# Strided products, copies and sums of zeros appended behind the last result, on four engines

## The chip, the core and the metric

The kernel runs on one core of a Trainium2 chip. The metric is the device time of one execution in microseconds; the figure given for a kernel is the median of its runs. A profiled execution of the same program supplies the trace that is read below. Five engines work side by side, each with its own queue in program order: PE (TensorE: matmuls, with a weight load, PEld, ahead of each), DVE (VectorE), ACT (ScalarE), POOL (GpSimd) and SP (SyncE, which issues the transfers). They wait for each other through semaphores.

## The reference

Two layers of width 1024 over a sequence of 2048 are computed from separate inputs and laid side by side. The first is attention with 32 heads of 32, the second a Fourier mixing by four given DFT matrices:

```
qkv = transpose(reshape(x @ wqkv))                 # 3, heads, sequence, 32
p   = softmax(q @ k.T * 32 ** -0.5)
a   = reshape(transpose(p @ v)) @ wo

re  = x @ dft_hid_re.T
im  = x @ dft_hid_im.T
b   = dft_seq_re @ re - dft_seq_im @ im

out = concatenate([a, b], axis=-1)                 # 1, 2048, 2048
```

All inputs and the output are fp32.

## The kernel before

Every dense product is made of 128 x 512 tiles. An fp32 operand is split into a high and a low part in the type fp32r, which TensorE multiplies faster than plain fp32, and a product is the sum of three: high by high, low by high, high by low. `halves` makes the two parts (the high part by a copy on DVE, L501, or on ACT, L499; the low part by a subtraction on POOL or DVE, L504). `group` issues the matmuls of one accumulation (L414) into a PSUM tile that `bank` takes from the pools `psD` (tile name `pd`) or `psT`. The larger products are cut by a seven-product scheme, with sums and differences of blocks made by `fetch` (L479).

The order of all engines is written out by hand. The class `Plan` simulates the engines with given costs while the program is being emitted: every operation is an `Op` with an engine, a cost, what it waits for and a rank, and `start` emits it into its engine's queue when the simulated engine comes free. The main loop at the end of `tile_mha_fnet_kernel` draws PE's work from four sources (scores, transposed scores, products with v, and the dense groups that fill what is left); the other engines follow in `others`. All of this stands in a `manual_schedule`, so each engine's queue has exactly the order in which instructions were emitted. The semaphores are put in afterwards from the tiles that instructions read and write. The plan also keeps POOL's operations and those DVE operations that are marked `two` (copies between SBUF tiles, and sums with two SBUF operands) apart from each other where it can.

SBUF is handed out by name. The pool `big` has 20 places `slot0` to `slot19` of 128 x 2 x 512 floats; taking a place again waits for all that read or wrote its previous tile. The pool `pre` has, among others, three places with the tag `c` of 128 x 512 floats. The PSUM pools have two tiles each: `psD` and `psT` of 512 columns and `psS` of 1024, which held score tiles during attention.

At the end stands `project_end`. It finishes the last fourth of the output projection: for each of 16 row blocks n and both halves e of the columns, a group of six matmuls over the last two chunks g of the contraction, whose result `total` adds to a partial sum (L1474, on DVE, one operand in SBUF and one in PSUM) and stores (L1479). The stores go out on SP's queue. The very last result is added and stored in two halves, the second of them on ACT's queue. In this part the places are used so: with BASE = 10 the offset o is 5, so the weights `ENDS_B[6, 0]`, `[6, 1]`, `[7, 0]` and `[7, 1]` lie in slots 1, 2, 3 and 4, the activations `ENDS_A` in slots 16 to 19 and 5 to 8, and the partial sums of block n, two per place, in slots 9, 10, 11, 0 and 12 to 15 in turn. Slot 0 thus holds those of blocks 3 and 11. A store uses one of eight semaphores ("lanes") in turn; a later one of the same lane waits for the earlier to land.

After the main loop the rest of the plan is run out, the manual order is closed, and `op_pool` makes sure that the late pools exist. Then every engine drains, SP waits for all transfers, and the engines meet (all recorded with the line L2162).

Two other places are spoken of below: the warm-up at the start (L377 to L379), eight products of zeros into a PSUM tile that nothing reads, and the softmax sums of a head on DVE (L1923 to L1927), a short chain in which each operation reads what the one before it wrote.

```
def halves: high: copy raw -> hi (DVE L501 or ACT L499)
            low:  raw - hi       (POOL or DVE L504)
def total:  acc + psum (DVE L1474), store (SP, the last half ACT, L1479)
```

Of the kernel before, what the change touches and what calls it, by code (L numbers as in the profile page):

```python
# [8 lines left out]
F32 = mybir.dt.float32  # L9
F32R = mybir.dt.float32r  # L10
AF = mybir.ActivationFunctionType
ALU = mybir.AluOpType
# [4 lines left out]
P = 128  # L17
# [6 lines left out]
NB = 512  # L24
# [198 lines left out]
def kernel(  # L223
# [12 lines left out]
    nc = tc.nc  # L236
# [35 lines left out]
    big = ctx.enter_context(tc.tile_pool(name="big", bufs=1, side="right"))  # L272
# [13 lines left out]
    pre = ctx.enter_context(tc.tile_pool(name="pre", bufs=1, reuse_waits="tile"))  # L286
# [34 lines left out]
    psS, psT, psD = (pools[n] for n in ("psS", "psT", "psD"))  # L321
# [60 lines left out]
    op = pl.op  # L382
# [1425 lines left out]
    def op_pool():  # L1808
        if "op" not in late:
            att().release()  # L1810
            qk0.release()
            late["atl"].release()
            late["oph"] = ctx.enter_context(tc.tile_pool(name="oph", bufs=1, side="right", reuse_waits="tile"))
            late["op"] = ctx.enter_context(tc.tile_pool(name="op", bufs=1, reuse_waits="tile"))
        return late["op"]
# [238 lines left out]
    while nf < len(fills) or any(place[n] < len(s) for n, s in streams.items()):  # L2054
# [18 lines left out]
        for n, (o, h, k) in heads.items():  # L2073
# [8 lines left out]
            if n == "V":  # L2082

                near = any(m in heads and heads[m][0].left == 0 and heads[m][0].ready + LATE < pl.now + NEAR and not (m == "S" and held) for m in "ST")
# [29 lines left out]
        if ok:  # L2114
            n = min(ok)[1]
# [10 lines left out]
        t = min(times)  # L2126
# [3 lines left out]
    while True:  # L2130
        pl.others()
        t = pl.next_time()
        if t > 1e17:
            break
        pl.now = max(t, pl.now + 1e-3)
    guard.__exit__(None, None, None)
    op_pool()

# [27 lines left out]
```

## Time and profile before

| | us |
|---|---|
| median of 3 runs | 2922.96 |
| lowest, highest run | 2922.64, 2923.09 |
| the profiled execution | 2929.45 |
| its span, first to last instruction | 2927.7 |
| PE busy | 2904.0 |
| DVE busy | 2386.5 |
| ACT busy | 2373.3 |
| POOL busy | 1241.3 |

The granted TensorE clock was 0.999 of full speed. The profiled execution is 6.5 us above the median, and 1.75 us of it lie outside the span. In the views below, the timeline gives the start in microseconds from the start of the span, the duration, the engine, the line, the operation with its output and inputs, its count, and in brackets the idle time of the engine before it with what ended it. Neighbouring instructions of one kind are merged into one row. The view of one line or one tile gives the count, the shortest, median and longest duration in nanoseconds, and the first and last start. An engine name with a q (SPq, ACTq) is the engine's sequencer: waits, drains and the issue of transfers.

### The profile page before, as it was taken

To read this page: it belongs to the slowest core of one execution; us is meant where nothing else is said; L and a number is where in the kernel's file an instruction comes from. 1 tells how busy PE (TensorE), PEld (TensorE's weight loads), DVE (VectorE), ACT (ScalarE), POOL (GpSimd) and SP (SyncE) were. 2 spreads that over 40 slices of the span, in tenths; PEclk is the share of its full clock that TensorE was granted. 3 is DMA by queue.
4 is the path that set the end of the run, shared out by engine and by line. 5 is a ranking of instruction groups with operands and counts; after the bars stand their busy time and mean duration, and the time that the engine had idled before them with its cause. 6 is when DMAs were issued, how large, how long until landed. Compare 5 with 4: busy or idle time off the path is not lost.

```text
span 2927.7 us, 47039 instructions
## 1 busy us (share of the span) xinstructions
PE 2904.0 (99%) x14728; PEld 2107.2 (72%) x14728; DVE 2386.5 (82%) x3251; ACT 2373.3 (81%) x4509; POOL 1241.3 (42%) x975
## 2 busy tenths in 40 slices
PE   9999999999999999999999999999999999999999
PEld 8887776777667777777676677667667777777777
DVE  7679888788788887788888898888988788788745
ACT  5348898888888888988999898898889888888741
POOL 2325534142233433337655456666675352243200
PEclk9999999999999999999999999999999999999999
DMA  9989978697789988867899776887876665677558
GB/s 345 349 298 328 314 225 272 222 346 269 268 289 339 309 297 287 291 213 218 291 348 333 226 223 216 276 272 229 271 229 208 204 180 181 193 246 226 188 191 287
DMA packets 485844, 768.18 MB, mean 262 GB/s; under 512 B 120382, under 2 KB 153406, under 8 KB 485470
## 3 DMA queue, kind: packets, MB, share of 16 engines
q1 hardware_dynamic: 485452, 765.04, 79.4%
q8 instruction: 119, 1.95, 0.3%
q14 instruction: 129, 1.06, 0.1%
q10 hardware_dynamic: 144, 0.13, 0.0%
HBM read 511.74 MB, written 253.25 MB: 261 GB/s over the span
## 4 chain that ended last, share of the span: by engine, by line
PE 75%; DMA 4%; DVE 1%; ACT 1%; SPq 0%; issue 0%; POOL 0%; DVEq 0%; ACTq 0%; POOLq 0%
PE pd L414 34%; PE psT L1975 14%; PE pd L1994 13%; PE psS L1853 13%; PE psT L414 2%; ACT psS L1862 1%; DVE negm L1859 1%; DMA qs<-m_d 1%; DMA slot<-in_ct 0%; DMA g<-in_ct 0%; DMA hl<-ha_d 0%; ACT pt L1979 0%; DMA m_d<-lt 0%; DMA ha_d<-slot 0%; DMA g<-g_d 0%
## 5 line engine op out<-in xcount | busy, mean ns | idle before, releaser
L414 PE MATMUL pd<-slot,hl 128*128 128x512 f32 x5028 | 1446.7, 390 | 4.2 <-DMA hl<-ha_d 1.4
L1979 ACT ACTIVATE pt<-psT 128x512 f32<-128x512 f32 x2048 | 1191.5, 668 | 260.7 <-PE psT L1975 258.5
L1859 DVE TENSOR_REDUCE negm<-psS 128x1 f32<-128x1024 f32 x1024 | 1240.7, 1221 | 198.3 <-PE psS L1853 190.1
L1862 ACT ACTIVATE psS<-psS,negm 128x1024 f32<-128x1024 f32 x1024 | 1189.2, 1161 | 47.4 <-DVE negm L1859 44.5
L414 PEld LDWEIGHTS pd<-slot,hl 128*128 128x128 f32 x5028 | 943.6, 188 | 204.8 <-DVE negm L1859 2.7
L1975 PE MATMUL psT<-qs,ks 128*128 128x512 f32 x2048 | 802.4, 395 | 4.4 <-DMA qs<-m_d 3.2
L1975 PEld LDWEIGHTS psT<-qs,ks 128*128 128x128 f32 x2048 | 382.2, 188 | 160.0 <-issue 53.0
L1853 PE MATMUL psS<-ks,qs 128*128 128x512 f32 x1552 | 473.1, 391 | 4.2 <-ACT psS L1862 4.2
L1994 PE MATMUL pd<-pt,vt 128*32 128x512 f32 x4096 | 460.9, 596 | 1.2 <-DVE e L723 0.9
L1853 PEld LDWEIGHTS psS<-ks,qs 128*128 128x128 f32 x1552 | 289.5, 188 | 69.1 <-ACT psS L1862 11.0
L504 POOL TENSOR_TENSOR slot<-raw,slot 128x512 fp32r<-128x512 f32 x153 | 196.2, 1291 | 316.1 <-DVE slot L501 116.6
L1994 PEld LDWEIGHTS pd<-pt,vt 128*32 128x32 f32 x4096 | 123.4, 110 | 285.1 <-issue 268.3
L504 POOL TENSOR_TENSOR slot<-slot,slot 128x512 fp32r<-128x512 f32 x183 | 234.3, 1292 | 206.1 <-DVE slot L501 54.5
L1862 ACT ACTIVATION_READ_ACCUMULATOR psS<-psS,negm 128x1 f32 x1024 | 287.0, 280 | 0.0
L504 POOL TENSOR_TENSOR hl<-raw,hl 128x512 fp32r<-128x512 f32 x122 | 156.8, 1289 | 257.4 <-DVE hl L501 84.7
L479 POOL TENSOR_TENSOR raw<-raw,g 128x512 f32<-128x512 f32 x119 | 153.3, 1291 | 226.6 <-ACT pt L1979 31.3
L414 PE MATMUL pd<-slot,slot 128*128 128x512 f32 x780 | 210.6, 389 | 0.1
L414 PEld LDWEIGHTS pd<-slot,slot 128*128 128x128 f32 x780 | 146.4, 188 | 30.9 <-DVE e L723 0.4
L1853 PE MATMUL psS<-ks,qx 128*128 128x512 f32 x496 | 151.0, 394 | 3.3 <-ACT psS L1862 3.2
L479 DVE TENSOR_TENSOR raw<-raw,g 128x512 f32<-128x512 f32 x141 | 103.3, 738 | 23.6 <-DMA g<-in_ct 6.6
L1853 PEld LDWEIGHTS psS<-ks,qx 128*128 128x128 f32 x496 | 91.7, 188 | 34.6 <-issue 9.2
L479 POOL TENSOR_TENSOR slot<-slot,slot 128x512 f32<-128x512 f32 x79 | 102.1, 1302 | 27.5 <-DVE slot L479 11.3
(140 smaller groups left out, 2167.6 us busy)
## 6 DMA issues: line engine op xcount, KB each, us to landing
hl<-ha_d SPq DMA_DIRECT2D x134, 512.0 KB
slot<-in_ct SPq DMA_DIRECT2D x144, 256.0 KB
qk_d<-e SPq DMA_DIRECT2D x52, 512.0 KB
qs<-qk_d SPq DMA_DIRECT2D x128, 192.0 KB
ks<-qk_d SPq DMA_DIRECT2D x128, 192.0 KB
raw<-g_d SPq DMA_DIRECT2D x96, 256.0 KB
ha_d<-hl SPq DMA_DIRECT2D x42, 512.0 KB
raw<-in_ct SPq DMA_DIRECT2D x80, 256.0 KB
```

The costliest lines, as they stand in the source:

```text
L414: nc.tensor.matmul(box["ps"], a[1]((a[0].hi, a[0].lo)[u]()), b[1]((b[0].hi, b[0].lo)[v]()), start=k == 0, stop=k == n - 1)
L479: (nc.gpsimd if e == "POOL" else nc.vector).tensor_tensor(out=dest(), in0=dest() if a is None else a.get(), in1=other["q"] if "q" in other ...
L504: (nc.gpsimd if e == "POOL" else nc.vector).tensor_tensor(out=lo(), in0=raw(), in1=f(hi()), op=ALU.subtract)
L1853: nc.tensor.matmul(p[:, i * NB : i * NB + NB], (QX[0] if own else QS[h % 2])[:, qt * P : qt * P + P], KS[h % 2][:, c * 1024 + i * NB : c * ...
L1859: nc.vector.tensor_reduce(out=ST["negm"][:, c, qt : qt + 1], in_=box["p"], axis=AX.X, op=ALU.max, negate=True)
L1862: nc.scalar.activation(box["p"], box["p"], AF.Exp, bias=ST["negm"][:, c, qt : qt + 1], accum_out=ST["sums"][:, c, qt : qt + 1])
L1975: nc.tensor.matmul(box["p"], KS[h % 2][:, t * P : t * P + P], QS[h % 2][:, j * NB : j * NB + NB], start=True, stop=True)
L1979: nc.scalar.activation(box["t"], box["p"], AF.Exp)
L1994: nc.tensor.matmul(po["p"][j * DH : j * DH + DH, :], VT[h][:, k, :], box["t"], start=(k == t0), stop=(k == t), tile_position=(0, j * DH),)
```

## The change

Behind the last planned operation, still inside the manual order, the changed kernel emits work on tiles of zeros. Nothing before it is altered, and none of what it computes is read by anything that reaches the output.

- POOL fills six tiles with zeros: two of 512 columns in the places `c` (`zl`, `zs`), and four of 1024 columns in slots 0 to 3 (`zu`, `zw`, `zv`, `zx`, in this order). A third `c` tile is taken and not used.
- PE makes two plain products into the two `psT` tiles (`pa`, `pb`), of 128 columns of `zw` with 512 of `zu`, and then 42 products into half of a `psS` tile (`pc`): for each of seven ways to step through the same 512 columns of `zu` six products that accumulate.
- POOL makes eight subtractions on `zs` and `zl`, two rounds of four.
- ACT makes twelve copies into the first half of `zv`, two rounds of six, four from PSUM (`pb`) and two from SBUF (`zs`).
- DVE works twenty times on the first half of `zx`, two rounds of ten: four sums with `pa` in PSUM, four copies from `zs`, two subtractions from `zs`.

All of these handle 128 x 512 floats. Within a round the first operation of a kind is plain, the others step through one or both operands. The views mean, for 512 columns: `two` and `duo` and `near` go through the tile in its own order, written as two or three dimensions; `odd` takes every second column, first the even ones and then the odd; `even` takes every second pair; `far` takes column 0, 256, 1, 257 and so on.

```diff
@@ -2133,6 +2133,58 @@
             break
         pl.now = max(t, pl.now + 1e-3)
+    zl, zs, zo = (pre.tile([P, NB], F32, name="c", tag="c", bufs=3) for _ in range(3))
+    zu, zw, zv, zx = (big.tile([P, 2 * NB], F32, name=n, tag=n) for n in ("slot0", "slot1", "slot2", "slot3"))
+    for z in (zl, zs, zu, zw, zv, zx):
+        nc.gpsimd.memset(z, 0.0)
+    pa, pb, pc = psT.tile([P, NB], F32, name="psT"), psT.tile([P, NB], F32, name="psT"), psS.tile([P, 1024], F32, name="psS")
+    u, w = (z.bitcast(F32R) for z in (zu, zw))
+    b = w[:, 0:P]
+    for p in (pa, pb):
+        nc.tensor.matmul(p, b, u[:, 0:NB], start=True, stop=True)
+    m = u[:, 0:NB]
+    forms = [
+        (b, m.rearrange("p (i n) -> p n i", i=2)),
+        (b, m.rearrange("p (i n e) -> p n i e", i=2, e=2)),
+        (b, m.rearrange("p (n i e) -> p n e i", i=2, e=4)),
+        (b, m.rearrange("p (n i e) -> p n e i", i=2, e=2)),
+        (b, m.rearrange("p (n i e) -> p n e i", i=4, e=4)),
+        (b, m.rearrange("p (n i e) -> p n e i", i=2, e=8)),
+        (b, m.rearrange("p (i n e) -> p n i e", i=2, e=4)),
+    ]
+    for x, y in forms:
+        for i in range(6):
+            nc.tensor.matmul(pc[:, 0:NB], x, y, start=(i == 0), stop=(i == 5))
+    two, odd = (lambda t: t.rearrange("p (i n) -> p i n", i=2)), (lambda t: t.rearrange("p (n i) -> p i n", i=2))
+    far = lambda t: t.rearrange("p (i n) -> p n i", i=2)
+    near = lambda t: t.rearrange("p (n i) -> p n i", i=2)
+    duo = lambda t: t.rearrange("p (i n e) -> p i n e", i=2, e=2)
+    even = lambda t: t.rearrange("p (n i e) -> p i n e", i=2, e=2)
+    z0, z1, z2 = zu[:, 0:NB], zv[:, 0:NB], zx[:, 0:NB]
+    r2 = z2.bitcast(F32R)
+    for k in range(2):
+        nc.gpsimd.tensor_tensor(out=zl, in0=zs, in1=zl, op=ALU.subtract)
+        nc.gpsimd.tensor_tensor(out=two(zl), in0=odd(zs), in1=two(zl), op=ALU.subtract)
+        nc.gpsimd.tensor_tensor(out=near(zl), in0=far(zs), in1=near(zl), op=ALU.subtract)
+        nc.gpsimd.tensor_tensor(out=far(zl), in0=near(zs), in1=far(zl), op=ALU.subtract)
+    for k in range(2):
+        nc.scalar.activation(z1, pb, AF.Copy)
+        nc.scalar.activation(two(z1), odd(pb), AF.Copy)
+        nc.scalar.activation(far(z1), near(pb), AF.Copy)
+        nc.scalar.activation(duo(z1), even(pb), AF.Copy)
+        nc.scalar.activation(two(z1), odd(zs), AF.Copy)
+        nc.scalar.activation(near(z1), far(zs), AF.Copy)
+    for k in range(2):
+        nc.vector.tensor_tensor(out=z2, in0=z2, in1=pa, op=ALU.add)
+        nc.vector.tensor_tensor(out=two(z2), in0=two(z2), in1=odd(pa), op=ALU.add)
+        nc.vector.tensor_tensor(out=far(z2), in0=far(z2), in1=near(pa), op=ALU.add)
+        nc.vector.tensor_tensor(out=duo(z2), in0=duo(z2), in1=even(pa), op=ALU.add)
+        nc.vector.tensor_copy(z2, zs)
+        nc.vector.tensor_copy(two(z2), odd(zs))
+        nc.vector.tensor_copy(near(z2), far(zs))
+        nc.vector.tensor_copy(far(z2), near(zs))
+        nc.vector.tensor_tensor(out=two(z2), in0=odd(zs), in1=two(z2), op=ALU.subtract)
+        nc.vector.tensor_tensor(out=near(z2), in0=far(zs), in1=near(z2), op=ALU.subtract)
     guard.__exit__(None, None, None)
     op_pool()
```

## The prediction

> **What bounds the kernel now.** I read the page first, then the timeline of the last stretch, engine by engine, and last the rows of the closing lines. The page:
>
> ```profile
> span 2927.7 us, 47039 instructions
> ...
> PE 2904.0 (99%) x14728; PEld 2107.2 (72%) x14728; DVE 2386.5 (82%) x3251; ACT 2373.3 (81%) x4509; POOL 1241.3 (42%) x975
> ```
>
> TensorE is busy from end to end, so work added beside it would have to fit into the others' gaps. But the added instructions stand behind everything else in each engine's queue, and what counts is only how the program ends. The timeline of the end (start, duration, engine, line, what):
>
> ```profile
> 2877.90 1.29 POOL L504 TENSOR_TENSOR slot<-raw,slot 128x512 fp32r<-128x512 f32 x1 [57.13 <-DVE slot L504]
> ...
> 2882.13 0.63 ACT L499 ACTIVATE slot<-raw 128x512 fp32r<-128x512 f32 x1 [2.46 <-PE psT L414]
> ...
> 2918.65 2.88 PE L414 MATMUL psT<-slot,slot 128*128 128x512 f32 x12
> ...
> 2921.37 1.52 PE L414 MATMUL pd<-slot,slot 128*128 128x512 f32 x6
> 2921.57 0.69 DVE L1474 TENSOR_TENSOR slot<-slot,psT 128x512 f32<-128x512 f32 x1 [0.67 <-PE psT L414]
> 2922.93 0.75 DVE L1474 TENSOR_TENSOR slot<-slot,pd 128x256 f32<-128x256 f32 x2 [0.67 <-PE pd L414]
> 2923.71 0.37 ACTq L1479 DMA_DIRECT2D out<-slot  x1
> ```
>
> POOL is through at 2879.2, ACT computes nothing after 2882.8, PE ends at 2922.9, DVE at 2923.7; then two stores go out. Twelve matmuls start in 2921.37 - 2918.65 = 2.72 us, 0.227 us each. The closing lines and the store queues (minimum/median/maximum ns, then first and last start):
>
> ```profile
> L1479 ACTq EVENT_SEMAPHORE  x1: 3845/3845/3845, 2917.6 to 2917.6; - x1
> ...
> L2162 SPq EVENT_SEMAPHORE  x8: 17/28/260, 2926.3 to 2927.6; - x8
> ...
> L2162 SPq DRAIN  x3: 7/7/7, 2926.9 to 2927.2; - x3
> L2162 POOLq EVENT_SEMAPHORE  x4: 17/17/17, 2927.0 to 2927.6; - x4
> ```
>
> From 2926.3 SP sees the last stores landed, at 2926.9 it drains, and from 2927.0 all engines meet, which takes 0.75 us up to 2927.7. So an engine may work until 2926.9 unseen; beyond that every microsecond counts whole, and the end is that of the last engine plus 0.75.
>
> **When the added work can start.** Nothing is removed or moved; six fills, 44 matmuls, 12 ACT copies, 20 DVE and 8 POOL operations are added. POOL's fills come first, in its order: two tiles of 512 (the `c` buffers, whose last users lie far back: hidden behind the final groups), then four of 1024 in slots 0 to 3. Slot 0 held the accumulators of row block 11; its second half leaves with the ninth store ahead of ACT's, on the same one of eight lanes, so ACT's wait above tells when it has landed: 2917.6 + 3.85 = 2921.4. Slots 1 and 3 (weights read by the last but one group) are free at 2921.5, slot 2 at 2922.9. The price of a fill, with the unread warm-up products beside it:
>
> ```profile
> L336 POOL MEMSET qx<- x1: 519/519/519, 204.3 to 204.3; 32x512 f32 x1
> ...
> L336 POOL MEMSET ks<- x1: 1806/1806/1806, 208.8 to 208.8; 32x2048 f32 x1
> ...
> L337 POOL MEMSET ks<- x1: 1802/1802/1802, 210.7 to 210.7; 2x2048 f32 x1
> ...
> L379 PE MATMUL pd<-c x8: 628/628/794, 1.5 to 4.6; 128*128 128x512 f32 x8
> ```
>
> The partition count is without effect (2048 elements take 1.80 on 32 partitions and on 2), so 1024 elements take 0.52 + (1.80 - 0.52)/3 = 0.95, some 0.9 when they follow closely. zu runs from 2921.5, zw is done at 2923.4, zv at 2924.3, zx at 2925.2. Queued behind them: PE's first two products wait for zw (it stands idle 0.6 us), ACT for zv, DVE for zx, POOL's own subtractions for all. So PE's strided forms start at 2923.5 + 2 x 0.227 = 2924.0, ACT at 2924.3, DVE and POOL at 2925.2.
>
> **What each engine needs**, by the rows of the same shape:
>
> ```profile
> L1474 DVE TENSOR_TENSOR slot<-slot,psT x16: 686/687/689, 2882.1 to 2921.6; 128x512 f32<-128x512 f32 x16
> ...
> L501 DVE CAST hl<-raw x149: 384/420/1486, 158.8 to 2865.8; 128x512 fp32r<-128x512 f32 x149
> ...
> L504 POOL TENSOR_TENSOR hl<-raw,hl x122: 1260/1289/1302, 213.0 to 2747.3; 128x512 fp32r<-128x512 f32 x122
> ...
> L499 ACT ACTIVATE slot<-raw x88: 615/633/900, 148.0 to 2882.1; 128x512 fp32r<-128x512 f32 x88
> ```
>
> Each added operation writes or reads what the one before it wrote. The next rows show what that costs, and what a strided read costs on DVE: L1924 reads a tile of 2 x 16 floats as 16 pairs, so neighbours in its stream lie 64 bytes apart.
>
> ```profile
> 404.63 0.19 DVE L1923 TENSOR_TENSOR tt<-tt,sums 128x32 f32<-128x32 f32 x1
> 404.85 0.19 DVE L1924 TENSOR_REDUCE rec<-tt 128x16 f32<-128x32 f32 x1
> 405.07 0.25 DVE L1925 RECIPROCAL rec<-rec 128x16 f32<-128x16 f32 x1
> ...
> L1924 DVE TENSOR_REDUCE rec<-tt x32: 186/188/191, 250.0 to 2745.9; 128x16 f32<-128x32 f32 x32
> ...
> L1859 DVE TENSOR_REDUCE negm<-psS x1024: 1175/1224/1228, 68.8 to 2740.7; 128x1 f32<-128x1024 f32 x171
> ...
> L1474 DVE TENSOR_TENSOR slot<-slot,pd 128x256 f32<-128x256 f32 x2 | 0.8, 418 | 0.7 <-PE pd L414 0.7
> ```
>
> L1474 at 256 and at 512 elements (0.418 and 0.687) gives 1.05 ns per element; with it the contiguous reduction L1859 leaves 1.224 - 1.075 = 0.149 fixed, and 32 elements would take 0.149 + 0.034 = 0.183. L1924 takes 0.188, where two slots per element would make 0.217: its stride costs next to nothing. It starts at 404.85, some 0.03 after 404.63 + 0.19, the operation that it depends on; I add 0.035 to each dependent operation on DVE and ACT, 0.05 on POOL.
>
> ACT: 12 x 0.67 = 8.0, to 2932.3. Were every element twice as dear (0.43 more each) it would be 2937.5; I take the first, and neither ends last.
>
> PE: 42 x 0.227 = 9.5, to 2933.5, if a strided stream costs what a plain one does. No row shows one. The lower bound is 0.227, the upper the dearest row of this shape, 0.628 (L379, the program's first products), 26.4 in all. I take the lower, the row of the same stage.
>
> DVE alone: per round four sums with PSUM 4 x 0.72, four copies 4 x 0.455, two subtractions 2 x 0.72, so 6.15; two rounds 12.3. By L1924 I add nothing for strides (the upper bound, each interleaved stream at twice its elements, is in a rival below).
>
> POOL alone: a fill of 512 is 0.52, a subtraction 1.29, so each of the two streams it reads costs about 0.385. The four with `far` operands read one stream in jumps; at half rate that gives 1.68, with a jumping store or both reads 2.06, without any penalty 1.29. I take 1.68, between the ends, because POOL, unlike DVE, pays for every stream. Sum 4 x 1.29 + 4 x 1.68 = 11.9.
>
> **Together they cost more than apart.** DVE copies between SBUF tiles, and its subtractions of two SBUF tiles, don't run beside a POOL subtraction:
>
> ```profile
> 1243.07 1.29 POOL L479 TENSOR_TENSOR slot<-slot,slot 128x512 f32<-128x512 f32 x1 [0.74 <-DMA slot<-in_ct]
> ...
> 1243.78 1.12 DVE L479 TENSOR_TENSOR slot<-slot,slot 128x512 f32<-128x512 f32 x1 [1.24 <-DMA slot<-in_ct]
> ```
>
> ```profile
> 2131.67 2.67 POOL L479 TENSOR_TENSOR slot<-slot,g 128x512 f32<-128x512 f32 x2 [3.41 <-DMA g<-in_ct]
> 2134.30 1.46 POOL L1048 TENSOR_TENSOR e<-c,e 128x512 f32<-128x512 f32 x1
> 2135.72 1.46 POOL L479 TENSOR_TENSOR slot<-slot,g 128x512 f32<-128x512 f32 x1
> ```
>
> ```profile
> 2134.07 1.97 DVE L501 CAST slot<-slot 128x512 fp32r<-128x512 f32 x2
> ...
> L479 POOL TENSOR_TENSOR slot<-slot,slot x79: 1265/1292/1770, 1215.2 to 2184.1; 128x512 f32<-128x512 f32 x79
> ```
>
> The DVE subtraction lasts 1.12 and ends 0.54 after POOL's. Of the two casts the second can't follow the first: POOL's next operation gets in between, takes 1.46 instead of 1.29, and the cast ends 0.28 after it. So they alternate; a copy holds POOL up for 0.17, a subtraction for 0.48 (1.77 - 1.29). L1474's sums read one operand from PSUM and take their plain 0.687, and I let the added ones run beside POOL.
>
> Round one, from 2925.2: the four PSUM sums (2.9) lie beside POOL's first three operations (1.34 + 1.34 + 1.68 = 4.4). Then DVE's six wait for one POOL operation each: copy, +0.18 + 1.68 = 6.26; copy, +0.18 + 1.29 = 7.73; copy, 9.20; copy, +0.18 + 1.68 = 11.06; subtraction, +0.48 + 1.68 = 13.22, POOL's end; the last subtraction ends 0.57 later, 13.8. Round two runs alone: 6.15, to 19.9. DVE ends at 2925.2 + 19.9 = 2945.1, 11 us behind PE; plus 0.75 the span is 2945.9, 18.2 more than 2927.7. The profiled execution took 2929.45, 6.5 above the median 2922.96; I add the 18.2 to the median: **2941.1**. Its own range, with POOL's stride between 1.29 and 2.06 (four times 0.39 either way) and a microsecond for the starts, is 2938.5 to 2944.
>
> **Rivals.**
> *A stride costs everywhere* (20%). DVE's 32 elements in L1924 are few; a long stream could fall behind. At two slots per element in the jumping streams DVE loses 0.53 per sum or subtraction and 0.27 per copy, 2.7 where it isn't hidden, POOL another 1.5: 2945.3; with PSUM's stride-two reads doubled too, 2946.4. Against it: 0.188 above. The Trainium skill's page "Advanced Engine Details and Errata", section "SBUF Cachelines", speaks for it: SBUF is read in 16-byte lines, and accesses that each fall on another line pay. L1924's 64-byte jumps fall on another line each and show no such payment, so by this trace the rule doesn't bind DVE; PE's four forms that change line with each element would come under it.
> *PE ends last* (12%). Four of the seven forms (24 matmuls) jump between distant or neighbouring groups with each element. At m times 0.227, PE ends at 2924.0 + 18 x 0.227 + m x 5.45; twice is 2939.0, still hidden; it decides from m = 3.1. With all 42 at 0.628 it is 2950.4, span 2951.1, 2946.4 in time. For it: no row excludes it; against: three is much.
> *No alternation* (14%). If strided copies take DVE's plain way, or POOL doesn't bar them, each engine needs only its own sum: DVE 2925.2 + 12.3 = 2937.5, POOL 2925.2 + 11.9 + 8 x 0.05 = 2937.5, span 2938.3, 2933.5. Against it stand the rows with 1.12 and 1.46, though all with contiguous operands.
> *Not slower* (4%). None of the results is read; if the build leaves out what nobody reads, the program is the old one, 2923. It decides as soon as DVE's work beyond 2923.7 shrinks below 2926.9 - 2923.7 = 3.2. L379, eight products into a tile that nothing reads, stands in the trace, which speaks against it.
>
> **How the numbers follow.** The forecast has 50%. The range 2932 to 2948 takes in the lone engines below and both stride cases above; outside remain 4% at 2923 and a part of PE's and the strides' upper tails. A measurement here tells 0.2%, 5.8 us, from no change; every case but the last lies 10 or more above, so slower has 0.95, within 0.2% 0.04, faster 0.01.
>
> **What would show it.** In the changed profile: POOL's fill of slot 0 starts near 2921.5 and that of slot 3 ends near 2925.2; DVE's last subtraction ends near 2945 and the meeting of engines follows within a microsecond; DVE's first-round copies last 1.4 to 2 us with POOL operations between them, its second-round copies 0.42; PE is through before 2940, ACT before 2935; nothing ahead of 2921 differs. The forecast is wrong if PE's rows stand last, if first-round copies take 0.42, if second-round `far` rows take well over 0.69, or if the fills start later than 2922.

## The result, and the profile after

The changed kernel took 2939.86 us, the median of three runs (2935.97 to 2944.62), against 2922.96 before: a ratio of 1.0059 with a 95% interval of 1.0041 to 1.0077, or 16.9 us more. The forecast was 2941.1.

First the head of the page of the changed kernel:

```profile
span 2938.1 us, 47178 instructions
...
PE 2913.5 (99%) x14772; PEld 2114.1 (72%) x14772; DVE 2405.4 (82%) x3271; ACT 2381.0 (81%) x4521; POOL 1258.5 (43%) x989
```

There are 139 instructions more, and PE is still at 99%: the page's shares cannot show what happened. The end of the timeline does (start, duration, engine, line, what, idle time before it and what ended it):

```profile
2913.37 0.96 POOL L2139 MEMSET slot<- 128x1024 f32 x1 [39.61 <-DMA out<-slot]
2914.53 0.95 POOL L2139 MEMSET slot<- 128x1024 f32 x1 [0.21 <-PE psT L414]
...
2915.89 1.84 POOL L2139 MEMSET slot<- 128x1024 f32 x2 [0.41 <-PE pd L414]
...
2916.55 0.75 DVE L1474 TENSOR_TENSOR slot<-slot,pd 128x256 f32<-128x256 f32 x2 [0.67 <-PE pd L414]
...
2916.80 10.55 PE L2157 MATMUL psS<-slot,slot 128*128 128x512 f32 x42
...
2917.77 0.69 DVE L2178 TENSOR_TENSOR slot<-slot,psT 128x512 f32<-128x512 f32 x1 [0.47 <-POOL slot L2139]
...
2921.08 1.09 DVE L2182 COPY slot<-c 128x512 f32<-128x512 f32 x1
...
2921.96 1.52 POOL L2169 TENSOR_TENSOR c<-c 128x512 f32<-128x512 f32 x1
2922.20 1.57 DVE L2183 COPY slot<-c 128x512 f32<-128x512 f32 x1
...
2923.56 1.33 POOL L2166 TENSOR_TENSOR c<-c 128x512 f32<-128x512 f32 x1
...
2926.19 0.77 ACT L2176 ACTIVATE slot<-c 128x512 f32<-128x512 f32 x1
...
2928.09 1.74 POOL L2169 TENSOR_TENSOR c<-c 128x512 f32<-128x512 f32 x1
2928.59 1.78 DVE L2187 TENSOR_TENSOR slot<-c,slot 128x512 f32<-128x512 f32 x1
2930.41 0.69 DVE L2178 TENSOR_TENSOR slot<-slot,psT 128x512 f32<-128x512 f32 x1
...
2931.85 1.06 DVE L2180 TENSOR_TENSOR slot<-slot,psT 128x512 f32<-128x512 f32 x1
...
2934.12 0.43 DVE L2183 COPY slot<-c 128x512 f32<-128x512 f32 x1
...
2935.05 0.63 DVE L2185 COPY slot<-c 128x512 f32<-128x512 f32 x1
...
2936.44 0.69 DVE L2187 TENSOR_TENSOR slot<-c,slot 128x512 f32<-128x512 f32 x1
```

The real work ends with L1474 at 2917.30 (its two halves start at 2916.55). In the profile before it ended later, at 2923.68, so spans must not be subtracted here: executions of one kernel differ by several us (the three runs of the changed kernel lie 8.7 us apart, and the profiled execution before was 6.5 above its median). If all of those 6.5 us lie ahead of the last L1474, a median execution of the kernel before ends it near 2917.2, an estimate, and that is where the changed kernel ends it too. What can be compared is the stretch from the end of the last L1474 to the end of the span. Before it is 2927.66 - 2923.68 = 3.98; after, 2938.08 - 2917.30 = 20.78. The difference, 16.8, agrees with the 16.9 of the medians. All stretches below are taken in this way.

Of the 20.78, DVE waits 0.47 for the last fill, works from 2917.77 to 2937.13 (19.37 with its gaps of 0.03), and 0.95 follows. PE is through ten microseconds earlier (2916.80 + 10.55), ACT at 2926.96, POOL at 2929.83. DVE's two rounds do the same ten operations; the first takes 2930.41 - 2917.77 = 12.64, the second 6.72. In round one the copy L2183 takes 1.57 and ends 0.28 after POOL's L2169, which started before it; in round two, with POOL done, the same copy takes 0.43.

The chain of waits, asked for the last 38 us, says the same by its own route (start, length, what):

```profile
2915.15 0.69 PE pd L414 x3
2915.84 0.05 issue
2915.89 1.85 POOL slot L2139 x2
2917.74 0.02 issue
2917.77 0.70 DVE slot L2178
```

From there it is DVE alone down to L2187 at 2936.44. Note "x3": the last fills were let go by the third of the last group's six products, not by its end. And the closing line, as for the kernel before (shortest, median, longest in ns; first and last start):

```profile
L2214 SPq EVENT_SEMAPHORE  x8: 17/28/17752, 2918.9 to 2938.0; - x8
...
L2214 SPq DRAIN  x3: 7/7/7, 2937.3 to 2937.6; - x3
```

SP's longest wait was 0.26 before; now it stands 17.75 us until DVE's last operation.

### The profile page after: what moved, and what is told of

Read it like the earlier page. It is cut to its first block, busy times and chain, and to the rows that moved or that the text cites. A ratio compares the mean times of both kernels' runs of the same rounds, so it can differ in the third digit from the quotient of the medians.

```text
span 2938.1 us, 47178 instructions
## 1 busy us (share of the span) xinstructions
PE 2913.5 (99%) x14772; PEld 2114.1 (72%) x14772; DVE 2405.4 (82%) x3271; ACT 2381.0 (81%) x4521; POOL 1258.5 (43%) x989
## 3 DMA queue, kind: packets, MB, share of 16 engines
q14 instruction: 130, 1.06, 0.1%
## 4 chain that ended last, share of the span: by engine, by line
PE 90%; DMA 4%; DVE 3%; ACT 2%; issue 1%; SPq 0%; POOL 0%; DVEq 0%; ACTq 0%; POOLq 0%
PE pd L414 41%; PE psT L1975 15%; PE psS L1853 15%; PE pd L1994 14%; PE psT L414 5%; ACT psS L1862 1%; DVE negm L1859 1%; ACT pt L1979 0%; DMA slot<-in_ct 0%; DMA g<-in_ct 0%; DMA qs<-m_d 0%; DMA ha_d<-slot 0%; DVE hl L501 0%; DMA vt<-v_d 0%; DMA qk_d<-e 0%
## 5 line engine op out<-in xcount | busy, mean ns | idle before, releaser
L414 PE MATMUL pd<-slot,hl 128*128 128x512 f32 x5028 | 1446.4, 390 | 3.2 <-DVE negm L1859 1.3
L1979 ACT ACTIVATE pt<-psT 128x512 f32<-128x512 f32 x2048 | 1192.0, 669 | 258.9 <-PE psT L1975 256.9
L414 PEld LDWEIGHTS pd<-slot,hl 128*128 128x128 f32 x5028 | 943.4, 188 | 203.1 <-POOL hl L504 1.9
L1975 PE MATMUL psT<-qs,ks 128*128 128x512 f32 x2048 | 802.6, 395 | 1.1 <-DMA qs<-m_d 0.6
L1975 PEld LDWEIGHTS psT<-qs,ks 128*128 128x128 f32 x2048 | 382.2, 188 | 158.0 <-issue 56.2
L1853 PE MATMUL psS<-ks,qs 128*128 128x512 f32 x1552 | 473.1, 391 | 3.9 <-ACT psS L1862 3.8
L1853 PEld LDWEIGHTS psS<-ks,qs 128*128 128x128 f32 x1552 | 289.5, 188 | 69.2 <-ACT psS L1862 11.1
L414 PE MATMUL pd<-slot,slot 128*128 128x512 f32 x780 | 210.6, 389 | 0.0
L414 PEld LDWEIGHTS pd<-slot,slot 128*128 128x128 f32 x780 | 146.4, 188 | 30.5 <-DVE e L723 0.2
L1853 PE MATMUL psS<-ks,qx 128*128 128x512 f32 x496 | 151.2, 395 | 3.4 <-ACT psS L1862 3.3
L1853 PEld LDWEIGHTS psS<-ks,qx 128*128 128x128 f32 x496 | 91.6, 188 | 35.2 <-issue 9.2
```

What stands on the lines that cost most here:

```text
L414: nc.tensor.matmul(box["ps"], a[1]((a[0].hi, a[0].lo)[u]()), b[1]((b[0].hi, b[0].lo)[v]()), start=k == 0, stop=k == n - 1)
L1853: nc.tensor.matmul(p[:, i * NB : i * NB + NB], (QX[0] if own else QS[h % 2])[:, qt * P : qt * P + P], KS[h % 2][:, c * 1024 + i * NB : c * ...
L1975: nc.tensor.matmul(box["p"], KS[h % 2][:, t * P : t * P + P], QS[h % 2][:, j * NB : j * NB + NB], start=True, stop=True)
L1979: nc.scalar.activation(box["t"], box["p"], AF.Exp)
```

## The experiments

Theory: the end is DVE's, which shares turns with POOL in round one; the start is set by POOL's fills. Rivals: another engine or the strides themselves set the end.

**No subtractions on POOL.** POOL's eight subtractions are left out.

```diff
     for k in range(2):
-        nc.gpsimd.tensor_tensor(out=zl, in0=zs, in1=zl, op=ALU.subtract)
-        nc.gpsimd.tensor_tensor(out=two(zl), in0=odd(zs), in1=two(zl), op=ALU.subtract)
...
-    for k in range(2):
         nc.scalar.activation(z1, pb, AF.Copy)
```

> The changed kernel without POOL's eight subtractions; fills, products, ACT copies and DVE's 20 operations stay. Measured from the end of the last real sum (L1474) to the end of the span, 20.8 us in the changed kernel's profile. If DVE's first round is long because it takes turns with POOL, it falls from 12.6 to the second round's 6.8 and the stretch becomes 15.0 us, with first-round copies at 0.43 (0.63 for the one that stores in jumps). If the first round is long for another reason (its first use of the tiles, the start), it stays at 20.8. If PE set the end, it stays too.

Median 2934.37 of four runs (2933.25 to 2939.23) against 2921.43 before on that chip; 1.0049 times (1.0032 to 1.0065). The stretch is 15.28. DVE's timeline in round one:

```profile
2916.86 0.69 DVE L2173 TENSOR_TENSOR slot<-slot,psT 128x512 f32<-128x512 f32 x1 [0.67 <-POOL slot L2139]
...
2920.16 0.43 DVE L2177 COPY slot<-c 128x512 f32<-128x512 f32 x1
2920.62 0.43 DVE L2178 COPY slot<-c 128x512 f32<-128x512 f32 x1
2921.08 0.44 DVE L2179 COPY slot<-c 128x512 f32<-128x512 f32 x1
2921.56 0.72 DVE L2180 COPY slot<-c 128x512 f32<-128x512 f32 x1
2922.31 0.69 DVE L2181 TENSOR_TENSOR slot<-c,slot 128x512 f32<-128x512 f32 x1
```

Copies that took 1.09, 1.57, 1.39 and 1.67 beside POOL take 0.43 to 0.72 without it, subtractions 0.69 instead of 1.64 and 1.78. The stretch is 20.78 - 15.28 = 5.5 us shorter, although DVE started 0.20 later in this execution (0.67 behind the last L1474 instead of 0.47). Round one itself went from 12.64 to 6.90, so the alternation with POOL costs 5.7 us; nothing else was taken away.

**No work on DVE.** DVE's twenty operations are left out.

```diff
-    for k in range(2):
-        nc.vector.tensor_tensor(out=z2, in0=z2, in1=pa, op=ALU.add)
...
-        nc.vector.tensor_tensor(out=near(z2), in0=far(zs), in1=near(z2), op=ALU.subtract)
     guard.__exit__(None, None, None)
```

> The changed kernel without DVE's 20 operations. If the end is DVE's alone, the next engine takes it over: POOL, undisturbed, 8 operations of 1.27 to 1.45 with 0.08 between them, 11.2 us from its last fill, and the stretch from the last real sum to the end becomes 12.3 us. If POOL is not slowed by DVE its rows stay as they are and it is 13.3. If the end is PE's, it stays near 20.8.

One run: 2928.69, stretch 12.57. POOL's first round, undisturbed, from its timeline:

```profile
2914.75 1.26 POOL L2166 TENSOR_TENSOR c<-c 128x512 f32<-128x512 f32 x1
2916.09 1.31 POOL L2167 TENSOR_TENSOR c<-c 128x512 f32<-128x512 f32 x1
2917.49 1.42 POOL L2168 TENSOR_TENSOR c<-c 128x512 f32<-128x512 f32 x1
2918.99 1.44 POOL L2169 TENSOR_TENSOR c<-c 128x512 f32<-128x512 f32 x1
```

POOL is now last, its last operation ending 11.79 behind the last L1474; PE ends at 10.06 and ACT at 9.65, as they did with DVE at work. So DVE alone makes the difference between 12.6 and 20.8. On POOL an operand in jumps costs about 0.15 (1.26 to 1.42), a far cry from the 0.39 that I had put. Its dependent operations are 0.08 apart (1.26 after 2914.75 ends at 2916.01, the next starts at 2916.09); between DVE's copies the plain L2166 took 1.33 in the changed kernel, 0.07 more, where the prediction had let a copy hold POOL up for 0.18.

**The start.** DVE's tile is moved from slot 3 to the third place `c`, which has long been free, and is filled ahead of the slots.

```diff
-    for z in (zl, zs, zu, zw, zv, zx):
+    for z in (zl, zs, zo, zu, zw, zv):
...
-    z0, z1, z2 = zu[:, 0:NB], zv[:, 0:NB], zx[:, 0:NB]
+    z0, z1, z2 = zu[:, 0:NB], zv[:, 0:NB], zo
```

> The changed kernel with DVE's tile in the third c place, filled long before, instead of slot 3, so that one fill less stands ahead of POOL's subtractions and DVE needn't wait for it. If the start is set by the fills, DVE starts 0.45 us earlier, at once behind the last real sum, POOL 0.9 earlier, and the stretch of 20.8 us becomes 19.9. If the start is set by something else, it stays.

Median 2936.62 of four (2934.03 to 2941.76), 1.0053 times (1.0038 to 1.0068); stretch 19.95. From its timeline:

```profile
2911.55 0.75 DVE L1474 TENSOR_TENSOR slot<-slot,pd 128x256 f32<-128x256 f32 x2 [0.67 <-PE pd L414]
...
2912.22 0.68 DVE L2178 TENSOR_TENSOR c<-c,psT 128x512 f32<-128x512 f32 x1
```

DVE goes on without a wait in the row, 0.55 earlier against the last L1474 than in the changed kernel, and the stretch is 0.83 shorter. The fill in slot 3 did set DVE's start; the remaining 0.28 comes from a shorter first copy (0.74 instead of 1.09). It started later within POOL's operation and ended, as in the changed kernel, just under 0.3 after it.

**All plain on ACT, DVE and POOL.** The operations stay, every operand is read and written in its own order.

```diff
-    two, odd = (lambda t: t.rearrange("p (i n) -> p i n", i=2)), (lambda t: t.rearrange("p (n i) -> p i n", i=2))
...
+    two = odd = far = near = duo = even = lambda t: t
```

> ACT's, DVE's and POOL's added operations all read and write plainly; their number, their shapes and PE's forms stay. Read as the stretch from the end of the last real sum to the end of the span, 20.78 us with the changed kernel. Theory (on DVE only the two stores in jumps of a round cost anything, 0.37 the sum and 0.20 the copy, and POOL loses about 0.05 to 0.17 per operation with an interleaved operand): DVE's second round falls from 6.76 to 6.2, its third and eighth rows read 0.69 and 0.43, its first round falls by about 0.6 (0.42 in the sum, the rest by POOL's shorter turns), POOL's undisturbed rows stand near 1.27; stretch 19.6 (19.2 to 20.0). Rival A (strides cost nothing beside the alternation, and the long rows had another cause): the third and eighth rows of round two stay at 1.06 and 0.63 and the stretch at 20.6 or more. Rival B (the interleaved reads cost too, hidden in rows that I read as plain): DVE's rows of all forms fall, round two to below 6.0, stretch below 19.0.

One run: 2938.39, stretch 19.97. The timeline:

```profile
2917.57 0.69 DVE L2174 TENSOR_TENSOR slot<-slot,psT 128x512 f32<-128x512 f32 x1 [1.01 <-POOL slot L2139]
...
2919.01 0.69 DVE L2176 TENSOR_TENSOR slot<-slot,psT 128x512 f32<-128x512 f32 x1
...
2929.43 0.69 DVE L2174 TENSOR_TENSOR slot<-slot,psT 128x512 f32<-128x512 f32 x1
...
2933.70 0.43 DVE L2181 COPY slot<-c 128x512 f32<-128x512 f32 x1
...
2934.89 0.69 DVE L2183 TENSOR_TENSOR slot<-c,slot 128x512 f32<-128x512 f32 x1
```

DVE started late in this execution (1.01 behind the last L1474 instead of 0.47), which hides part of the gain. Its own work went from 19.37 to 2935.58 - 2917.57 = 18.01: round one 11.86 instead of 12.64, round two 6.15 instead of 6.72. The 0.57 of round two is the two stores in jumps: L2180's sum (1.06 against 0.69; it also reads its SBUF operand in these jumps) and L2185's copy (0.63 against 0.43). Reads from SBUF in jumps or by every second column, and from PSUM by every second column or pair, cost DVE nothing: those rows are 0.69 and 0.43 in both kernels. DVE read nothing from PSUM in jumps. The stretch missed the centre of what was expected, 19.6, by the late start; without it, it would be 19.43. Rivals A and B fall: in round two the rows did change, and only those two.

**PE's streams.** Seven other forms: plain and jumping, each with one and with six different weights; every second column; four streams 128 apart; neighbouring blocks of four interleaved.

```diff
+    jump = lambda t: t.rearrange("p (i n) -> p n i", i=2)
+    step = lambda t: t.rearrange("p (n i) -> p i n", i=2)
+    quad = lambda t: t.rearrange("p (i n) -> p n i", i=4)
+    swap = lambda t: t.rearrange("p (n i e) -> p n e i", i=2, e=4)
+    bs = [w[:, k * P : k * P + P] for k in range(6)]
+    forms = [([b] * 6, m), (bs, m), ([b] * 6, jump(m)), (bs, jump(m)), (bs, step(m)), (bs, quad(m)), (bs, swap(m))]
     for x, y in forms:
         for i in range(6):
-            nc.tensor.matmul(pc[:, 0:NB], x, y, start=(i == 0), stop=(i == 5))
+            nc.tensor.matmul(pc[:, 0:NB], x[i], y, start=(i == 0), stop=(i == 5))
```

> The changed kernel with other streams in the 42 products: plain with one weight tile, plain with six, jumps of 256 columns with one and with six weight tiles, every second column, four streams 128 apart, and neighbours swapped in groups of 4. The end is DVE's and stays at 20.8 us behind the last real sum, since PE is 10 us ahead. Spacing of starts: if the step pattern sets it, plain is 0.227 and jumps 0.216 with one weight tile and with six. If 0.216 comes from repeating one weight tile, plain with one is 0.216 as well and jumps with six 0.227. If jumping costs, as a line rule would have it, every form but plain is above 0.227.

One run: 2939.05, stretch 21.41 (20.8 was expected; DVE started 0.59 later than in the changed kernel). PE's busy time by windows, cut at the start of each form, so that the length of a window is the time of its six products; the count in the row also holds products that reach over a border:

```profile
core 0: us, PE busy (x) PEld busy (x), PEclk, DMA share, GB/s
2915.65:2917.03 1.38, 1.38 (x7) 1.13 (x6) 1.00 0.92 332
2917.03:2918.39 1.36, 1.36 (x8) 1.13 (x6) 1.00 0.14 46
2918.39:2919.68 1.29, 1.29 (x7) 1.13 (x6) 1.00 0.06 13
2919.68:2920.98 1.30, 1.30 (x8) 1.14 (x6) 1.00 0.00 0
2920.98:2923.67 2.69, 2.69 (x7) 1.23 (x6) 1.00 0.00 0
2923.67:2925.40 1.73, 1.73 (x7) 1.17 (x6) 1.00 0.00 0
2925.40:2926.70 1.30, 1.30 (x7) 0.95 (x5) 1.00 0.00 0
```

Divided by six: plain 0.230 and 0.227, jumping 0.215 and 0.217, every second column 0.448, four streams 0.288, blocks of four 0.217. The weights make no difference, the step pattern does. A stream that goes 0, 256, 1, 257 is 5% *faster* than one in order; why, no run shows. Of the changed kernel's own seven forms, the same view gives these windows for the second (pairs from two streams) and the fifth (every fourth column within blocks of sixteen):

```profile
2918.09:2920.08 1.99, 1.99 (x8) 1.17 (x6) 1.00 0.32 100
...
2922.77:2924.38 1.61, 1.61 (x7) 1.13 (x6) 1.00 0.00 0
```

That is 0.332 and 0.268 for a product.

**Using it.** That was worth a try on the real products. About 10,600 of the kernel's matmuls are of this shape: L414 (6528), and in attention L1853 and L1975 (2048 each). In a first version all three read their moving operand (the streamed one) in jumps, and every reader for which the order matters takes the even columns of the result first and then the odd, which restores it. The maximum and the sum over L1853's scores need no order and stay as they were. Nothing is left out.

```diff
+def jump(t):
+    return t.rearrange("p (i n) -> p n i", i=2)
...
-                    nc.tensor.matmul(box["ps"], a[1]((a[0].hi, a[0].lo)[u]()), b[1]((b[0].hi, b[0].lo)[v]()), start=k == 0, stop=k == n - 1)
+                    nc.tensor.matmul(box["ps"], a[1]((a[0].hi, a[0].lo)[u]()), jump(b[1]((b[0].hi, b[0].lo)[v]())), start=k == 0, stop=k == n - 1)
...
-                nc.vector.tensor_tensor(out=C.at()[:, c], in0=C.at()[:, c], in1=ps()[:, c], op=ALU.add)
+                nc.vector.tensor_tensor(out=tw(C.at(), c), in0=tw(C.at(), c), in1=od(ps(), c), op=ALU.add)
```

> The kernel before with the moving operand of all 10,624 products of L414, L1853 and L1975 read in jumps (column 0, 256, 1, 257, ...), and the PSUM result read back with every second column where its order matters; nothing is left out. If the 0.011 us per product seen on zeros holds on real data and with changing weights, starts are 0.216 apart instead of 0.227, 10,624 x 0.011 = 117 us less on TensorE; with 75 to 90% of the chain on TensorE and the hand-made order kept, 60 to 105 us of it reach the end, 2815 to 2862. If the gain belongs to zeros or to idle neighbours, spacing stays at 0.227 and the time at 2921. If reading every second PSUM column costs the DVE or ACT, their rows at L1474 and L1979 rise above 0.69 and 0.67 and eat it up.

Median 2868.60 of four (2867.68 to 2871.37) against 2923.36 on that chip: 0.982 times (0.9804 to 0.9837), 55 us less. At 11 ns for each of 10,624 products it would have been 117; 60 to 105 were expected, so the gain fell short of the range. The distances from the start of each product to the next one's, summed in the traces by line (us), show where the rest stayed:

```
         before   jumping   11 ns each would give
L414     1494.6   1434.6    1422.8
L1853     477.1    463.7     454.6
L1975     489.5    502.4     467.0
```

The median distance is 0.216 on all three lines, but L1975, the products whose exponentials ACT takes, grew: 741 of them stand over 0.26 from the next, 168 before. Its weight loads in the groups of the page (lines here are 18 higher than before; L1993 is L1975, L1997 the exponentials):

```profile
L1993 PEld LDWEIGHTS psT<-qs,ks 128*128 128x128 f32 x2048 | 381.8, 187 | 261.0 <-ACT pt L1997 139.1
```

The same group in the profile before, with the names and shapes kept apart as here:

```profile
L1975 PEld LDWEIGHTS psT<-qs,ks 128*128 128x128 f32 x2048 | 382.2, 188 | 160.0 <-issue 53.0 <-ACT pt L1979 9.5 <-DMA qs<-m_d 5.9
```

Of the idle time there ACT's exponentials ended 9.5 us before, now 139.1. One reading is that the order, written out by a plan that still counts 0.2275 us for a product, asks for the next one before ACT is done with the last.

The stepped reading of PSUM costs DVE nothing (the median of L1474 is 0.687 in both kernels). For ACT it is not settled: its exponentials L1979 take 0.678 in the mean instead of 0.668, but those of the scores, which are read in order in both kernels, rose too, from 1.161 to 1.184. Some of the gain also goes at the end: behind the last sum the stretch is 6.90 instead of 3.98; SP's last store is issued 1.23 after that sum there, and 0.30 ahead of it in the kernel before.

In a second version the plan's figure is the measured one, and nothing else changes.

```diff
-    MM, PV, SWITCH, TINY = 0.2275, 0.853, 0.40, 0.17
+    MM, PV, SWITCH, TINY = 0.2165, 0.853, 0.40, 0.17
```

> The same with the plan's cost of a product set from 0.2275 to 0.2165, so that the order is laid out for the faster TensorE. If the old order leaves TensorE waiting for transfers and for the other engines, this one is 5 to 30 us below the kernel with the old cost; if the order hardly matters, the two are within 5 us.

Median 2862.46 of four (2858.47 to 2865.26): 0.9796 times (0.9781 to 0.9811), 6.1 us below the first version. From its page:

```profile
span 2860.0 us, 46160 instructions
...
PE 84%; DMA 6%; ACT 4%; DVE 4%; issue 1%; POOL 1%; SPq 0%; DVEq 0%; POOLq 0%; ACTq 0%
```

PE still sets most of the time. L1975's products now lose less (491.6 us, 222 over 0.26), so the plan's figure was part of what stood in the way. The rest of the 117 us did not come back: L1975 is still 25 us above its 467.0, L414 and L1853 stay where they were (1434.6 and 465.0), the stretch behind the last sum is 7.0, and the granted clock was 0.995 here where the first version had 0.999; what that took was not separated. This version beats both kernels: 61 us less than the one before.

## Why the prediction was right, point by point

The mechanism held: the added work runs behind everything, DVE ends last, and its first round is stretched by turns with POOL. The terms, with times counted from the end of the last L1474 (2923.68 in the profile that the prediction used):

```
                          predicted   measured   off by
DVE's first operation       +1.52      +0.47     -1.05
DVE, round one              13.8       12.64     -1.2
DVE, round two               6.15       6.72     +0.57
from DVE's end to the end    0.75       0.95     +0.20
stretch                     22.2       20.78     -1.4
stretch less that before    18.2       16.8      -1.4
```

- *The start.* "zu runs from 2921.5", 2.2 ahead of the last L1474's end, was too late: it ran from 3.93 ahead, the DMA of slot 0 having landed earlier, and slot 2 became free within the last group, after its third product, not at its end. In the runs without subtractions, with plain operands and with other PE streams the fills ended 0.21, 0.55 and 0.60 later against the last L1474, and DVE started 0.20, 0.54 and 0.59 later.
- *Round one.* The alternation is shown by its removal (round one 5.7 us shorter). I had it 1.2 too long, because POOL's operations are shorter than I took them: the "at half rate that gives 1.68" of jumping reads was 1.42 undisturbed, near the lower bound 1.29. The eight subtractions came to 10.83 where DVE was idle, and I had 11.9; that is 1.1 of the 1.2. What I added for gaps and hold-ups, 13.22 - 11.9 = 1.3, is what they came to (12.13 from POOL's first subtraction to the end of its last, less 10.83), though not item by item: between dependent operations POOL leaves 0.08 and not 0.05, and the plain L2166 was held up by 0.07 and not 0.18.
- *Round two.* "By L1924 I add nothing for strides": right for every read, wrong for two stores per round. L1924 reads in jumps and stores in order; it said nothing of stores. With all operands plain, round two took 6.15, the figure of the prediction.
- *PE and ACT.* PE ended at +10.05 (predicted +9.8), ACT at +9.66 (predicted +8.6; its far stores took 1.10 and not 0.67). Both were hidden, as forecast. PE's 42 products took 10.55 where I had 9.5, and began 0.8 earlier; the one price of 0.227 stood for forms between 0.216 and 0.332.
- *Luck in the total.* The terms were off by 3.0 us taken singly and by 1.4 together, because round two and the end were too short where the start and round one were too long. The forecast of the median came out 1.2 us too high.

The rivals. *A stride costs everywhere* is refuted: reads are free on DVE, and what strides cost in all on DVE's path is 1.36 us, 0.57 of it in round two's stores. The rule of the Trainium skill that stood beside it, in "Advanced Engine Details and Errata", section "SBUF Cachelines" (accesses that each fall on another line of 16 bytes pay), does not sort these rows. On PE, three of the changed kernel's four forms that change the line with each element start 0.216 to 0.218 apart, less than the 0.227 of plain ones, and the fourth 0.268; the form that costs twice, every second column (0.448), still has two columns in each line. On DVE the reads that change the line are free, and the stores that do are the two that pay. *PE ends last* falls: no form comes near 3.1 times. *No alternation* falls by the first experiment. *Not slower* falls by the result: all the work is in the trace.

Of what was to show the forecast wrong, one sign came: of round two's rows with a far store the sum stood at 1.06, well over 0.69, and the copy at 0.63 instead of 0.43. Their 0.57 us was made up for by the terms of the opposite sign.

What stays open: why the stretch ahead of the end differs by several us between executions of the same kernel, why slot 0's store lands earlier or later against it, and why two distant streams are faster on PE than one in order. No run here was made for it.

## What to carry to other kernels

Compare tails from a common event, not whole spans: here the spans differed by 10.4 us where the tail had grown by 16.8. Price a strided operand by what it does, read or store, and on which engine; a row for one says nothing of the other. And once a stream is the bound, try its step pattern: products that read their operand in two distant streams started 5% closer together, DVE took the stepped result from PSUM at no cost, and 55 of the 117 us that this promised reached the end, 61 once the planned order knew the new price.

## What the runs showed of the hardware

- PE's fp32r products of 128 x 512 start 0.227 us apart in order, 0.216 with two streams 256 columns apart, 0.217 with blocks of four interleaved, 0.288 with four streams 128 apart, 0.448 with every second column; pairs from two streams (the second form of the changed kernel) took 0.332.
- DVE stores in jumps of 1 KB cost 0.37 us in a sum with PSUM and 0.20 in a copy of 512 columns; ACT's copy from PSUM goes from 0.60 to 1.10 with such a store, and its copy from SBUF from 0.63 to 0.77 with such a read; reads from SBUF in such jumps cost DVE nothing and add 0.15 to POOL's 1.27.
- A DVE copy between SBUF tiles that starts while a POOL subtraction runs ends 0.28 to 0.29 after it (L2182 to L2184 of the changed kernel; 0.53 where the copy stores in jumps, L2185); a copy alone takes 0.43.
